# A quarter of the first layer of chunks 1 to 6 by Strassen's identity, with leaky results on VectorE

## Chip, core and metric

The kernel runs on one core of a Trainium2 chip. The metric is the device time of one execution in microseconds, median of several runs. The granted TensorE clock was 1.00 in the profiled execution.

## What is computed

Attention with 16 extra keys and values ("beacons") in front, for 8 batches of 8 heads (576 queries of 64 numbers), then a two-layer network on the joined heads (4608 tokens of 512 numbers, inner width 2048) with a leaky activation between the layers:

```
scores = scale * q @ concat(beacon_k, k).T      # causal behind the beacons
a = softmax(scores)
x = (a @ concat(beacon_v, v)) as 4608 x 512
h = x @ w_in                                    # 512 -> 2048, "first layer"
g = maximum(0.01 * h, h)
out = g @ w_out                                 # 2048 -> 512, "second layer"
```

## The kernel before

Tokens go through the network in nine chunks of 512. `g` below is a pair of heads (32 of them, four to a batch). For each pair the kernel loads q and k, turns them by DMA (`turn_pair`, on SP's queue), computes scores in tiles of 512 columns (`stretch`, L314, three tiles to a `block`), exponentials on ScalarE (L329, L333), zeroes the masked triangles on GpSimd (`triangle`, L289) and multiplies by the values (`value`, L359). VectorE then reads the value bank: a reciprocal (L388) and a multiplication (L389) that writes `x_nat`; `x_turn` (L417 to L426, SP's queue) turns that into `xT`, the first layer's input.

The first layer of a chunk is 16 calls of `up`, one for each 128 columns of `w_in`. Each calls `moe1` (L431): 4 matmuls of 512 columns (L442; in chunk 4, where `xT` wraps around, 8 of 256) into one bank, and ScalarE writes the leaky result to `gT` (L450).

The second layer of chunks 1 to 8 is done by Strassen's identity in Winograd's form, with 7 products of quarter matrices in place of 8. `token_sums` makes sums of parts of `gT` on VectorE, in two slices of 4 column groups (each four operations of 128x1024, run through `add_due` at L785); `weight_sums` makes those of `w_out` (L468 to L472). `down` calls `moe2` (L531), 14 calls to a chunk: two for each of the products 1, 4, 6, 2, 7, 5, 3, with 8 matmuls of 256 columns each (L544). `combine` (L563) adds the products up: ScalarE copies products 1, 4 and 5 out of their banks (L575), and VectorE does seven fp32 additions of 128x512 (L572). The buffers of `combine` (`p1`, `p4`, `p5`, `u2`, `u3`) exist once each. Two of the additions and one result are held back by two groups (`late`). `store` sends each quarter of the result to memory.

Chunks 7 and 8 (`TAIL` = 7) also do three quarters of the first layer by the same identity, in three rounds (`in_round`, L687): `in_product` (L651) computes one of seven products with 4 matmuls of 256 columns (L663). Their sums of weights are made by `w_in_sums` (L619) during chunk 6 and kept in `w_t` (for product 7 in place, in `w_in_sb`); their sums of `xT` by `x_in_sums` (L637).

The order of work is the program's own on every engine. The first eight pairs are written out as strings of steps (`run`, L930 to L938). After that a planner sorts events (blocks, values, turns, loads) by due time and puts groups of the network between them with `fill` (L767), which counts calls of `up` and `down`: a chunk's `up` calls start when its tokens are there, and from chunk 2 on they begin after the 14 `down` calls of the chunk before. `due` is a queue of VectorE operations that wait to be issued; each `up` and each `down` issues one of them (`add_due`).

All matmul results outside the score tiles go through the pool `ps_one`, four banks of 512 fp32 columns: the first layer's, the second layer's, the values' and the first of each block's three score tiles (which takes two banks). The other score tiles have the pool `ps_sc`. The banks of `ps_one` are handed out again in the order in which their last readers are issued.

Of the kernel before, what the change touches and what calls it, by code (L numbers as in the profile page):

```python
# [8 lines left out]
FP32 = mybir.dt.float32  # L9
# [6 lines left out]
def kernel(  # L16
# [93 lines left out]
    first_k = [  # L110
        sum_tile(2)[0:RP, 0:QK].bitcast(FP32).rearrange("p (i d) -> p i d", i=RI) for _ in range(2)
    ]
    k_nat0 = singles.tile([RP, RI, 2, D], BF16, name="k_nat0")
    bk_raw = singles.tile([128, B, D], FP32, name="bk_raw")
    bk = singles.tile([128, B, D], BF16, name="bk")

# [414 lines left out]
    def moe2(i, n2):  # L531
        if i == 0:
            moe2_plain(i, n2 // 4, n2 % 4)
            if n2 == NF - 1:
                weight_sums(1)
            return
        n, tile = PRODUCTS[n2 // 2], n2 % 2
        apart = i == NCH - 1 and n2 >= 10
        if tile == 0 or apart:
            banks["p"] = one_bank()  # L540
        acc = banks["p"]
        lo = 0 if apart else tile * HD
        for fc in range(HF):
            nc.tensor.matmul(  # L544
                out=acc[:, lo : lo + HD],
                lhsT=left(i, n, fc, tile),
                rhs=right(n, fc),
                start=(lo == 0 and fc == 0),
                stop=(fc == HF - 1),
                skip_group_check=True,  # L550
            )
        if apart:
            combine(i, n, acc[:, 0:HD], (tile, tile + 1))
        elif tile == 1:
            combine(i, n, acc, (0, 2))

    late = []

# [1 line left out]
        while late and (now or late[0][0] < done1[0] + done2[0]):  # L560
            late.pop(0)[1]()

    def combine(i, n, acc, tiles):  # L563
        lo, hi = tiles[0] * HD, tiles[1] * HD

        def part(name, new=False):
            if new and lo == 0:
                parts[name] = opool.tile([128, 512], FP32, name=name, bufs=1)
            return parts[name][:, lo:hi]

        def add(to, x, y):
            nc.vector.tensor_tensor(out=to, in0=x, in1=y, op=ADD)  # L572

        if n in (1, 4, 5):
            nc.scalar.copy(out=part(f"p{n}", True), in_=acc)  # L575
        if n == 6:
            add(part("u2", True), acc, part("p1"))
        elif n == 2:
            add(part("p1"), acc, part("p1"))
            store(i, 0, 0, tiles, part("p1"))  # L580
        elif n == 7:
            add(part("u3", True), acc, part("u2"))
            add(part("p4"), part("u3"), part("p4"))
            store(i, 1, 0, tiles, part("p4"))
        elif n == 5:
            u2, u3, p5 = part("u2"), part("u3"), part("p5")

            def rest():
                add(u3, u3, p5)
                store(i, 1, 1, tiles, u3)  # L590
                add(p5, u2, p5)

            late.append((done1[0] + done2[0] + 1, rest))
        elif n == 3:
            add_late(True)
            add(part("p5"), acc, part("p5"))
            store(i, 0, 1, tiles, part("p5"))

    def store(i, half, cols, tiles, c):
        t0 = i * 512 + half * HT + tiles[0] * 128  # L600
# [15 lines left out]
        for name, (t, lo) in zip(("p1", "p5", "u2", "u3", "c12", "c21", "c22"), temp_at)  # L616
    }

    def w_in_sums(n, lo=0, hi=ROUNDS, first=False):  # L619
        cols = slice(lo * 256, hi * 256)  # L620
        (b11, b21), (b12, b22) = (
            [w_in_sb[i][:, at : at + 2, cols] for at in (0, 2)] for i in range(2)
        )
        x, y = {5: (b12, b11), 6: (b22, w_t[5][:, :, cols]), 4: (b21, w_t[6][:, :, cols]), 7: (b22, b12)}[n]
        at = 0 if first else len(due)
        due[at:at] = [
            (TAIL - 1, dict(out=w_t[n][:, j, cols], in0=x[:, j], in1=y[:, j], op=SUB)) for j in range(2)
        ]

    def x_parts(i):  # L630
        at = i * 512 % (XR * S)
        assert at + 512 <= XR * S
        return [[xT[:, 2 * c : 2 * c + 2, at + r * HT : at + (r + 1) * HT] for c in range(2)] for r in range(2)]
# [16 lines left out]

    def in_product(i, n, r, bank, first):  # L651
        (a11, a12), (_, a22) = x_parts(i)
        x = {1: a11, 2: a12, 4: a22}.get(n)
        x = x_sums[i][n] if x is None else x
        for f in range(2):
            cols = slice(r * 256 + f, r * 256 + f + 255, 2)
            for j in range(2):
                if n in w_t:
                    w = w_t[n][:, j, cols]
# [12 lines left out]
    leaves = []  # L672

# [114 lines left out]
    def add_all(i):  # L788
        while due and due[0][0] == i:
            add_due()  # L790
# [123 lines left out]
    with order:  # L914
# [127 lines left out]
```

## Time and profile before

| what | value |
|---|---|
| time before, median of 3 runs | 326.06 us (324.29 to 326.34) |
| the profiled execution's own time | 325.64 us |
| its span, first to last instruction | 323.8 us |
| PE (TensorE) busy | 314.3 us, 97% of the span |
| PEld (its weight loads, beside the matmuls) | 219.1 us, 68% |
| DVE (VectorE) busy | 168.0 us, 52% |
| ACT (ScalarE) busy | 203.8 us, 63% |
| POOL (GpSimd) busy | 184.3 us, 57% |

L and a number is a line of the kernel. In groups of instructions the columns are line, engine, operation, output and inputs by the program's names, shapes, count, then busy microseconds and mean nanoseconds of one, then idle time of the engine just before them and what ended it. In a timeline the columns are start, duration, engine, line, operation, names, shapes and count, and in brackets the idle time before and what ended it. In a list of waits they are the waiting engine, tile and line, what it waited for, the total in microseconds, the number of times and the longest. In the strip of 40 slices each digit is the busy share of a slice in tenths.

### The profile page before, as it was taken

The page shows a single profiled execution, that of the slowest core. Times are in us where ns is not written, and L with a number is a line of the kernel's source. Part 1 is how long each engine was busy: PE and PEld are TensorE (multiplying, and loading weights), DVE is VectorE, ACT ScalarE, POOL GpSimd, SP SyncE. Part 2 cuts the span into 40 slices and gives each one's busy share as a digit, 9 for nine tenths or more (in the row PEclk, how much of TensorE's full clock was granted, in tenths as well). Part 3 has the DMA queues.
Part 4 walks back from the last instruction along what each step waited for, and adds up shares of the span by engine and source line. Part 5 has one row for each costly group of instructions (what it writes and reads, how often), then busy time and mean ns, then how long its engine had stood idle before and what let it go on. Part 6 is the DMA issues. An engine that isn't in the chain of part 4 may idle for free.

```text
span 323.8 us, 8701 instructions
## 1 busy us (share of the span) xinstructions
PE 314.3 (97%) x3468; PEld 219.1 (68%) x3494; DVE 168.0 (52%) x341; ACT 203.8 (63%) x346; POOL 184.3 (57%) x354
## 2 busy tenths in 40 slices
PE   7999999999999999999999999999999999999995
PEld 4575555444588557855788888656875697688784
DVE  3464245508255244444443454525464689577954
ACT  4968962387855786478746874687458547455510
POOL 8895868999996787659875977666221000000000
PEclk9999999999999999999999999999999999999999
DMA  8999999999999999999999999999222100200123
GB/s 137 129 189 192 124 214 140 169 177 188 135 152 160 216 138 129 114 186 97 141 176 174 99 143 119 188 128 129 44 81 82 26 2 32 75 25 2 65 67 130
DMA packets 155256, 39.78 MB, mean 123 GB/s; under 512 B 142368, under 2 KB 152480, under 8 KB 155216
## 3 DMA queue, kind: packets, MB, share of 16 engines
q0 software_dynamic: 99824, 18.54, 91.1%
q1 hardware_dynamic: 55120, 20.62, 38.3%
q8 instruction: 27, 0.44, 0.6%
q14 instruction: 13, 0.11, 0.1%
q10 hardware_dynamic: 272, 0.07, 0.1%
HBM read 37.22 MB, written 9.44 MB: 144 GB/s over the span
## 4 chain that ended last, share of the span: by engine, by line
PE 72%; DMA 14%; POOL 9%; ACT 3%; issue 1%; DVE 0%; POOLq 0%; ACTq 0%; SPq 0%
PE acc L442 24%; PE acc L544 19%; PE sc L544 11%; PE av L359 6%; PE sc L314 5%; PE acc L663 5%; DMA w_out_sb<-in_moe_w_out_dram 4%; DMA gsum<-in_k_dram 4%; POOL aT L289 3%; DMA k_nat<-in_k_dram 3%; DMA v_aug<-in_v_dram 2%; ACT aT L333 2%; DMA kT<-k_nat 2%; POOL gsum L158 1%; POOL v_aug L214 1%
## 5 line engine op out<-in xcount | busy, mean ns | idle before, releaser
L442 PE MATMUL acc<-xT,w_in_sb 128*128 128x512 bf16 (+1 forms) x537 | 116.5, 354 | 1.5 <-ACT aT L329 0.3
L450 ACT ACTIVATE gT<-acc 128x512 bf16<-128x512 f32 x124 | 70.8, 623 | 33.1 <-PE acc L442 32.6
L289 POOL TENSOR_SCALAR_AFFINE_SELECT aT<-aT 128x256 bf16<-128x256 bf16 (+2 forms) x160 | 59.7, 403 | 51.4 <-ACT aT L329 31.5
L442 PEld LDWEIGHTS <-w_in_sb 128*128 128x128 bf16 x560 | 51.7, 98 | 43.9 <-issue 2.9
L544 PEld LDWEIGHTS <-gT 128*128 128x128 bf16 x512 | 48.7, 98 | 7.7 <-issue 1.8
L333 ACT ACTIVATE aT<-sc 128x1024 bf16<-128x1024 f32 (+3 forms) x64 | 51.7, 892 | 0.0
L329 ACT ACTIVATE aT<-sc 128x512 bf16<-128x512 f32 (+3 forms) x64 | 29.0, 520 | 27.8 <-PE sc L314 27.8
L388 DVE RECIPROCAL rec<-av 128x6 f32<-128x6 f32 (+1 forms) x64 | 12.0, 187 | 65.0 <-PE av L359 64.4
L359 PEld LDWEIGHTS <-aT 128*128 128x128 bf16 (+1 forms) x960 | 36.9, 98 | 9.2 <-issue 1.4
L544 PEld LDWEIGHTS <-gsum 128*128 128x128 bf16 x384 | 36.5, 98 | 6.5 <-issue 0.4
L359 PE MATMUL av<-v_aug,aT 128*128 128x65 bf16 (+1 forms) x960 | 39.8, 194 | 0.8 <-DMA v_aug<-in_v_dram 0.4
L214 POOL DMA_DIRECT2D v_aug<-in_v_dram x40 | 34.1, 856 | 4.2 <-DMA w_in_sb<-in_moe_w_in_dram 3.8
L171 POOL DMA_DIRECT2D k_nat<-in_k_dram x48 | 34.8, 730 | 0.9 <-DMA w_out_sb<-in_moe_w_out_dram 0.3
L171 POOL DMA_DIRECT2D q_nat<-in_q_dram x48 | 34.8, 729 | 0.6 <-issue 0.4
L389 DVE TENSOR_TENSOR x_nat<-av,rec 128x384 bf16<-128x384 f32 (+1 forms) x64 | 31.4, 491 | 2.2
L544 PE MATMUL acc<-w_out_sb,gT 128*128 128x256 bf16 x240 | 28.9, 273 | 0.4 <-ACT gT L450 0.4
L276 ACT ACTIVATE aT<-sc 128x1024 bf16<-128x1024 f32 (+3 forms) x32 | 26.0, 874 | 4.7 <-PE sc L267 2.5
L314 PE MATMUL sc<-qT,kT 64*128 64x80 bf16 (+22 forms) x384 | 22.2, 250 | 0.3
L314 PEld LDWEIGHTS <-kT 64*128 64x128 bf16 x384 | 12.8, 94 | 11.2 <-issue 7.6
L544 PE MATMUL acc<-w_sum,gsum 128*128 128x256 bf16 x160 | 20.1, 273 | 0.0
L575 ACT COPY p<-acc 128x512 f32<-128x512 f32 x15 | 9.1, 604 | 16.8 <-PE acc L544 16.8
L785 DVE TENSOR_TENSOR gsum<-gT 128x1024 bf16<-128x1024 bf16 x16 | 11.0, 688 | 15.7 <-ACT gT L450 15.7
(95 smaller groups left out, 339.0 us busy)
## 6 DMA issues: line engine op xcount, KB each, us to landing
out_dram<-p SPq DMA_DIRECT2D x26, 256.0 KB, 3.2
q_nat<-in_q_dram POOLq DMA_DIRECT2D x48, 72.0 KB, 5.5
k_nat<-in_k_dram POOLq DMA_DIRECT2D x48, 72.0 KB, 5.3
v_aug<-in_v_dram POOLq DMA_DIRECT2D x24, 128.0 KB, 6.5
w_in_sb<-in_moe_w_in_dram POOLq DMA_DIRECT2D x2, 1024.0 KB, 12.4
w_out_sb<-in_moe_w_out_dram POOLq DMA_DIRECT2D x2, 1024.0 KB, 12.1
out_dram<-u SPq DMA_DIRECT2D x8, 256.0 KB, 2.7
gsum<-in_q_dram POOLq DMA_DIRECT2D x8, 144.0 KB, 7.1
```

The costliest lines, as they stand in the source:

```text
L171: nc.gpsimd.dma_start(out=t[:, :, par], in_=(q, k)[which][b, 2 * hp + par].rearrange("(t p) d -> p t d", p=NR),)
L214: nc.gpsimd.dma_start(out=dst[lo : ROWS[c], c, :, 0:D], in_=v[b, :, OFF[c] : OFF[c] + n].rearrange("h p d -> p h d"),)
L276: nc.scalar.activation(out=aT[:, :, c0 : c0 + w], in_=sc[:, :, 0:w], func=AF.Exp, scale=0.125)
L289: nc.gpsimd.affine_select(out=view, in_=view, compare_op=ALU.is_ge, fill=0.0, base=128 - n if lo == 0 else 0, channel_multiplier=-1, patte ...
L314: nc.tensor.matmul(out=(sc[par] if apart else sc[:, par])[:, at : at + b - a], lhsT=kT[ps_, c * 128 : (c + 1) * 128], rhs=qT[ps_, q0 : q0 ...
L329: nc.scalar.activation(out=probs[g][:, par, lo:hi], in_=sc[par][:, at : at + hi - lo], func=AF.Exp, scale=0.125)
L333: nc.scalar.activation(out=probs[g][:, :, lo:hi], in_=sc[:, :, at : at + hi - lo], func=AF.Exp, scale=0.125)
L359: nc.tensor.matmul(out=avv[:, n, 0 : D + 1], lhsT=aT[0 : ROWS[c], par, a0 : a0 + 128], rhs=va[0 : ROWS[c], c, 2 * hp + par, :], start=(c = ...
L389: nc.vector.tensor_tensor(out=x_nat[:, t0:t1].rearrange("p t e d -> p (t e) d"), in0=avv[:, :, 0:D], in1=rec[:, n0:n1, None].to_broadcast( ...
L442: nc.tensor.matmul(out=acc[:, lo:hi], lhsT=w_in_cols(fc, j), rhs=xT[:, j, x0 : x0 + hi - lo], start=(j == 0), stop=(j == NJ - 1), skip_gro ...
L450: nc.scalar.activation(out=gT[i][:, fc, :], in_=acc, func=AF.Prelu, alpha=0.01)
L544: nc.tensor.matmul(out=acc[:, lo : lo + HD], lhsT=left(i, n, fc, tile), rhs=right(n, fc), start=(lo == 0 and fc == 0), stop=(fc == HF - 1) ...
```

## The change

In chunks 1 to 6 the sixteen calls of `up` become twelve plain groups and four units (`mixed_unit`). The units do column groups 0, 1, 8 and 9 by the identity: products 1 and 4, then 6 and 2, then 7 and 5, then 3, each product 4 matmuls of 256 columns in a bank of `ps_one`. A unit is taken when the second layer of the chunk before is done and a plain group has gone between, or when four plain groups are left. The products are added up by `combine`, as in the second layer, and its results go through `leak`, one scalar_tensor_tensor on VectorE (0.01 times the value, maximum with the value) into `gT`. Four sums of `xT` per chunk are put into `due` at the chunk's first group; they are kept in the columns of `gT` that the last four plain groups write. The second layer's first slice of token sums is put into `due` after the last unit, the second after the last plain group.

The weight sums for these columns are made once, by `t2` at the end of the written-out steps (eight operations of 128x256), into a new tile `w_in_sum` (product 7 in place); `k_nat0` shares that tile. The tail's `w_in_sums` then leave out the first 256 columns, and its rounds take them from `w_in_sum`.

```diff
-    k_nat0 = singles.tile([RP, RI, 2, D], BF16, name="k_nat0")
+    w_in_sum = singles.tile([128, 3, 2, 256], BF16, name="w_in_sum")
+    k_nat0 = w_in_sum.rearrange("p n j f -> p (n j f)")[0:RP, 0 : RI * 2 * D].rearrange(
+        "p (i h d) -> p i h d", i=RI, h=2
+    )
...
-        if part == 0:
+        if part == 2:
+            for n in (5, 6, 4, 7):
+                w_in_sums(n, 0, 1)
+            add_all(TAIL - 1)
+        elif part == 0:
...
-            combine(i, n, acc, (0, 2))
+            combine(i, n, acc, (0, 2), store)
...
-    def combine(i, n, acc, tiles):
+    def combine(i, n, acc, tiles, put):
...
-            store(i, 0, 0, tiles, part("p1"))
+            put(i, 0, 0, tiles, part("p1"))
...
-    def w_in_sums(n, lo=0, hi=ROUNDS, first=False):
+    def w_in_sum_of(n, lo, hi):
+        if n != 7 and lo == 0:
+            assert hi == 1
+            return w_in_sum[:, (5, 6, 4).index(n)]
+        return w_t[n][:, :, lo * 256 : hi * 256]
+
+    def w_in_sums(n, lo=1, hi=ROUNDS, first=False):
...
     def x_in_sums(i):
         (a11, a12), (a21, a22) = x_parts(i)
-        s1, s2, s3, s4 = (
-            flat_a[t][:, lo : lo + X_COLS].rearrange("p (j t) -> p j t", j=2)
-            for t, lo in sum_at[4 * (i - TAIL) : 4 * (i - TAIL) + 4]
-        )
+        if i < TAIL:
+            at = [gT[i][:, fc] for fc in UPS[-4:]]
+        else:
+            at = [flat_a[t][:, lo : lo + X_COLS] for t, lo in sum_at[4 * (i - TAIL) : 4 * (i - TAIL) + 4]]
+        s1, s2, s3, s4 = (t.rearrange("p (j t) -> p j t", j=2) for t in at)
...
+    UPS = [2, 10, 3, 11, 4, 12, 5, 13, 6, 14, 7, 15]
+    UNITS = [(1, 4), (6, 2), (7, 5), (3,)]
+    ups_left, units_left, x_ops = {}, {}, {}
+
+    def leak(i, half, cols, tiles, c):
+        nc.vector.scalar_tensor_tensor(
+            out=gT[i][:, cols * HF : cols * HF + 2, half * HT : (half + 1) * HT],
+            in0=c.rearrange("p (f t) -> p f t", f=2),
+            scalar=0.01,
+            in1=c.rearrange("p (f t) -> p f t", f=2),
+            op0=ALU.mult,
+            op1=ALU.max,
+        )
+
+    def mixed_unit(i, n):
+        if n == 0:
+            ups_left[i], units_left[i] = list(UPS), list(UNITS)
+            gT[i] = gpool.tile([128, NF, 512], BF16, name="gT")
+            x_ops[i] = x_in_sums(i)
+            due.extend(x_ops[i])
+        ups, units = ups_left[i], units_left[i]
+        if units and at2[0] >= i and (len(ups) == 4 or len(ups) < len(UPS) - len(UNITS) + len(units)):
+            for p in units.pop(0):
+                while p in x_sums[i] and any(op is o for op in x_ops[i] for o in due):
+                    add_due()
+                bank = ps_one.tile([128, 512], FP32, name="acc", tag="one")
+                in_product(i, p, 0, bank, True)
+                combine(i, p, bank, (0, 2), leak)
+            if not units:
+                due.extend((i, op) for op in token_sums(i, 0, SLICE))
+        else:
+            moe1(i, ups.pop(0))
+            if not ups:
+                due.extend((i, op) for op in token_sums(i, SLICE, 2 * SLICE))
...
-        fc = n if i1 == 0 else n // 2 + n % 2 * HF
-        moe1(i1, fc)
+        mixed = 0 < i1 < TAIL
+        if mixed:
+            mixed_unit(i1, n)
+        else:
+            moe1(i1, n if i1 == 0 else n // 2 + n % 2 * HF)
         if (i1, n) == (TAIL - 1, 4 * (ROUNDS - 1) + 2):
-            w_in_sums(7, 0, ROUNDS - 1, first=True)
+            w_in_sums(7, 1, ROUNDS - 1, first=True)
             add_due()
...
-        if i1 and n % (2 * SLICE) == 2 * SLICE - 1:
+        if i1 and not mixed and n % (2 * SLICE) == 2 * SLICE - 1:
...
-        run("m7.1 m7.2 N9.1 u b8.2 b9.2 b10.2 b11.2 x6 v7.0 T9 v7.1 d d d N10.0 N10.1 d V2.0 V2.1 x7 t0 T10")
+        run("m7.1 m7.2 N9.1 u b8.2 b9.2 b10.2 b11.2 x6 v7.0 T9 v7.1 d d d N10.0 N10.1 d V2.0 V2.1 x7 t0 t2 T10")
```

More of the change, by code (lines that the diff above doesn't have):

```diff
@@ L552, in moe2 @@
         if apart:
-            combine(i, n, acc[:, 0:HD], (tile, tile + 1))
+            combine(i, n, acc[:, 0:HD], (tile, tile + 1), store)
         elif tile == 1:
-            combine(i, n, acc, (0, 2))
+            combine(i, n, acc, (0, 2), store)
     late = []
@@ L583, in combine @@
             add(part("p4"), part("u3"), part("p4"))
-            store(i, 1, 0, tiles, part("p4"))
+            put(i, 1, 0, tiles, part("p4"))
         elif n == 5:
@@ L589, in rest @@
                 add(u3, u3, p5)
-                store(i, 1, 1, tiles, u3)
+                put(i, 1, 1, tiles, u3)
                 add(p5, u2, p5)
@@ L596, in combine @@
             add(part("p5"), acc, part("p5"))
-            store(i, 0, 1, tiles, part("p5"))
+            put(i, 0, 1, tiles, part("p5"))
     def store(i, half, cols, tiles, c):
@@ L623, in w_in_sums @@
         )
-        x, y = {5: (b12, b11), 6: (b22, w_t[5][:, :, cols]), 4: (b21, w_t[6][:, :, cols]), 7: (b22, b12)}[n]
+        x, y = {
+            5: lambda: (b12, b11),
+            6: lambda: (b22, w_in_sum_of(5, lo, hi)),
+            4: lambda: (b21, w_in_sum_of(6, lo, hi)),
+            7: lambda: (b22, b12),
+        }[n]()
+        to = w_in_sum_of(n, lo, hi)
         at = 0 if first else len(due)
         due[at:at] = [
-            (TAIL - 1, dict(out=w_t[n][:, j, cols], in0=x[:, j], in1=y[:, j], op=SUB)) for j in range(2)
+            (TAIL - 1, dict(out=to[:, j], in0=x[:, j], in1=y[:, j], op=SUB)) for j in range(2)
         ]
     def x_parts(i):
-        at = i * 512 % (XR * S)
-        assert at + 512 <= XR * S
-        return [[xT[:, 2 * c : 2 * c + 2, at + r * HT : at + (r + 1) * HT] for c in range(2)] for r in range(2)]
+        at = [(i * 512 + r * HT) % (XR * S) for r in range(2)]
+        assert max(at) + HT <= XR * S
+        return [[xT[:, 2 * c : 2 * c + 2, at[r] : at[r] + HT] for c in range(2)] for r in range(2)]
     x_sums = {}
@@ L658, in in_product @@
                 if n in w_t:
-                    w = w_t[n][:, j, cols]
+                    w = w_in_sum_of(n, r, r + 1)[:, j, f : f + 255 : 2]
                 else:
```

## The prediction

> **What bounds the kernel now.** I read the page's first two parts, then TensorE's waits, then the instructions of TensorE and VectorE in the stretch where chunk 2's first layer runs (105 to 124 us), and last the groups by shape for durations.
>
> ```profile
> PE 314.3 (97%) x3468; PEld 219.1 (68%) x3494; DVE 168.0 (52%) x341; ACT 203.8 (63%) x346; POOL 184.3 (57%) x354
> ...
> PE   7999999999999999999999999999999999999995
> ...
> DVE  3464245508255244444443454525464689577954
> ```
>
> TensorE (PE) works in nearly every slice; VectorE (DVE) is half idle through the middle. PE's waits on other engines come to 4.1 us in all; the longest groups are:
>
> ```profile
> PE av L825 <- DVE blank L917: 1.1, 1, 1.1
> PE tp L243 <- DMA gsum<-in_q_dram: 0.8, 1, 0.8
> PE acc L519 <- DMA w_out_sb<-in_moe_w_out_dram: 0.5, 1, 0.5
> PE acc L544 <- ACT gT L450: 0.4, 2, 0.2
> ```
>
> So PE is the bound, and time is won only by fewer PE cycles, or lost by a wait put in front of PE. Whether VectorE's idle half is free where the change needs it is seen in chunk 2:
>
> ```profile
> 105.17 2.75 PE L442 MATMUL acc<-xT,w_in_sb 128*128 128x512 bf16 x11
> 107.76 0.53 PE L359 MATMUL av<-v_aug,aT 128*128 128x65 bf16 x12
> 108.13 1.89 PE L442 MATMUL acc<-xT,w_in_sb 128*128 128x512 bf16 x8
> 109.86 0.71 PE L359 MATMUL av<-v_aug,aT 128*128 128x65 bf16 x18
> 110.41 1.03 PE L442 MATMUL acc<-xT,w_in_sb 128*128 128x512 bf16 x4
> 111.37 0.83 PE L314 MATMUL sc<-qT,kT 64*128 64x400 bf16 x12
> ```
>
> ```profile
> 108.33 0.20 DVE L388 RECIPROCAL rec<-av 128x6 f32<-128x6 f32 x1 [2.27 <-PE av L359]
> ...
> 110.61 0.18 DVE L388 RECIPROCAL rec<-av 128x4 f32<-128x4 f32 x1 [1.49 <-PE av L359]
> 110.83 0.42 DVE L389 TENSOR_TENSOR x_nat<-av,rec 128x256 bf16<-128x256 f32 x1
> 115.89 0.69 DVE L785 TENSOR_TENSOR gsum<-gT 128x1024 bf16<-128x1024 bf16 x1 [4.64 <-ACT gT L450]
> ```
>
> VectorE's idle time stands in brackets: 2.27, 1.49 and 4.64 us, 8.4 us up to 115.9. The value results (L388, L389) free their bank only when VectorE has read them.
>
> **The change, part by part.** Durations:
>
> ```profile
> L785 DVE TENSOR_TENSOR aT<-xT 128x512 bf16<-128x512 bf16 x3 | 1.2, 416 | 0.0
> L572 DVE TENSOR_TENSOR p<-acc,p 128x512 f32<-128x512 f32 x10 | 6.9, 691 | 8.1 <-PE acc L544 7.9
> L575 ACT COPY p<-acc 128x512 f32<-128x512 f32 x15 | 9.1, 604 | 16.8 <-PE acc L544 16.8
> L450 ACT ACTIVATE gT<-acc 128x512 bf16<-128x512 f32 x124 | 70.8, 623 | 33.1 <-PE acc L442 32.6
> ```
>
> PE. Per chunk, 4 plain groups of 16 matmuls of 512 columns become 7 products of 4 matmuls of 256. From starts in the timeline, a plain group takes 108.13 to 109.86 for two, 0.867 each; eight 256-column matmuls take 0.875 (94.62 to 95.50). So 4 x 0.867 = 3.47 against 28 x 0.109 = 3.06: 0.41 us saved, 2.4 us in six chunks. That is all that can be won.
>
> Here the Trainium skill speaks against the change: "TensorE: Matmul & The Clock Gate", section "Back-to-back issue gap", gives sustained streams about 81 ns per matmul at 128 columns and 131 ns at 512, weight loads included. An estimate from these (98 ns at 256) makes 28 x 98 = 2.73 against 16 x 131 = 2.10 us, a loss of 3.8 us in six chunks. The rows above decide: 217 and 109 ns.
>
> ACT. Four leaky results (4 x 623 ns) become three copies (3 x 604): 0.7 us less per chunk. PE waited for ACT 1 us in all, so it is worth nothing by itself.
>
> VectorE, per chunk. Four token sums (416 ns, 1.66 us), seven fp32 adds (691 ns) and four leaky results with a scalar_tensor_tensor on 512 fp32 elements, which the trace does not show. Its nearest row is the fp32 add of the same shape, 0.69, which I take; below, the same rows start 0.60 apart when independent (101.24 to 101.88 and the like); above, two passes would be 1.38. Eleven such operations in a queue with their dependences (0.60 or 0.72 apart) take 7.4 us: with the sums 9 us, and all of it falls in the first 8 of a chunk's 16 groups.
>
> Where it falls. The planner counts groups, and its counts do not change, so order and interleaving stay as in the trace. There all 14 down products of chunk i-1 come before chunk i's first group (chunks 2 to 6), so the condition on the second layer holds at once: plain, (1,4), plain, (6,2), plain, (7,5), plain, (3), then eight plain. In chunk 1 the down products end after its fifth group, and the four units come in a row.
>
> A walk through chunk 2, on the trace's clock. VectorE: chunk 1's last add to 106.06; three sums to 107.27; head 13's first value half is ready at 108.35, to 109.13; fourth sum 109.45; (6,2) gives u2 110.05, p1 110.65, leaky 111.37; the second value half, ready at 110.65, now 111.92; (7,5) gives 112.52, 113.24, leaky 113.96; the late part 114.56, leaky 115.28, 115.88; (3) 116.60, leaky 117.32. PE finished (3) at 114.06: VectorE is 3.3 us behind, and the slice's second-layer sums, issued one per group, now stand in front of head 14's value: three to 119.33, value to 120.02. PE meets this at the four ps_one banks, which go round in the order in which their readers are issued. The score tile at 111.32 wants the bank of head 13's second half, free at 111.92: 0.65 lost. Head 14's value half and the next plain group lose 0.16 and 0.33 behind (7) and (3) (free 115.90 and 116.60). The plain group at 118.95 wants head 14's bank, free at 120.02: 1.1 lost. Sum 2.24, less the 0.41 saved: +1.8 us.
>
> The same walk by the same durations gives: chunk 1 +4.9 (four units in a row, two value halves behind them, and the 2.3 us weight sum of L472 just ahead), chunk 2 +1.8, chunk 3 +2.8, chunk 4 +2.3, chunk 5 +1.8, chunk 6 +1.8. Sum +15.4.
>
> Weight sums ("t2"): eight operations of 128x256 bf16, 282 ns by the group of the same shape on w_in_sb (L785, twice in the tail), 0.19 apart, 1.5 us, put between the sums of L468 to L470 and the copy at 61.63. That copy frees the bank that chunk 1's first group wants at 62.3: +0.7. Later the tail's sums shrink (six from 768 to 512 columns, 0.55 to 0.42; two from 512 to 256, 0.42 to 0.28): 1.1 us of VectorE, in the walk of chunk 6.
>
> Edits at no cost. Two scratch uses: the x sums lie in the gT columns of the last four plain groups, whose results ACT writes from about 120 us, 5 us after the products have read them; k_nat0 is read 40 us before w_in_sum is written. If a product were late there, ACT's results and then PE would wait for it. No DMA is added or moved. But x_turn's transposes wait in SP's queue for VectorE's x_nat, and behind them stand the next heads' qT and kT transposes (1.2 us each); a value 2 to 3 us late delays them as much. They are issued about two heads (15 us) ahead of use, which covers it; if not, each late microsecond is PE's. The tail's rounds only take their first quarter's weights from another tile: nothing.
>
> Sum: 15.4 + 0.7 = 16.1 us, on the profiled execution's 325.64 us (span 323.8): 341.7. The walk on the old order gives 1.6 us more of bank waits than the trace shows, so I take off 0.7: 341.0. The profiled run lies 0.4 below the median of 326.06, so the forecast is +15 us on that.
>
> **The rivals.** (1) The backlog is absorbed, the other side. PE loses nothing as long as VectorE frees a bank before it comes round, three allocations or about 2.6 us later. If the walk's lag of 3.3 to 5 us stays below that, only the saving remains: 325.64 - 2.4 = 323.2, with t2 and chunk 1 partly paid some 327. For it: at 262 to 280 us VectorE works without a gap and PE does not wait. Against: there the second layer's products lie in other banks, no value stands in VectorE's queue and the leaky results are ACT's.
>
> (2) The leaky operation is dear. At 1.38 us, 24 operations add 17 us of VectorE, and by the walk 14.6 us more of waits: 356. For it: one two-input sum (L472) took 2303 ns where three like it took 1215 to 1226. Against: that is still 1.1 ns per element, so 512 elements fit in 0.69.
>
> (3) VectorE slows under GpSimd, busy in 57% of the span. Sums of 691 ns reached 887 once. If all two-input operations took 0.89, the walk gives 4 us more: 345. Against: 10 of 11 of that group keep 0.68 to 0.69.
>
> (4) The change does not do what it says: the units come in a row in every chunk. Each chunk then costs chunk 1's 4.9: 325.6 + 29.4 + 0.7 = 356. Against: the trace's order of down and up groups.
>
> **How the numbers follow.** The forecast with (3) as its upper part 0.73; (1) 0.15; (2) and (4) together 0.08; half waits (banks freed sooner than walked, +5 to +8, 331 to 333) sit at the forecast's lower edge; 0.04 for what I have not seen. About 1% is what a measurement of this kernel can tell from no change: 322.8 to 329.3. (1) lies inside it, as 2.4 us is 0.7%, though near its lower end; of (1) and the unseen 0.04 I count 0.13 as same, 0.03 as faster and 0.03 as slower, which with 0.73 and 0.08 makes slower 0.84. The range 330 to 356 leaves out (1) and what lies beyond (2). The forecast's own range is 333 to 350.
>
> **What would show it.** Right: VectorE's busy time rises by about 55 us to 223; L442's matmuls fall by 96 of 512 columns or their halves; PE waits on x_nat (L389) and on L572's adds grow from 0.6 us to over 10, chiefly in the second quarter of each chunk's groups; ACT falls by 4 us; the tail from the last value on keeps its 67 us. Wrong: PE's waits stay under 3 us, the leaky row is far from 0.69, or chunk 1 does not lose the most.

## The result and the profile after

| what | value |
|---|---|
| time after, median of 6 runs | 337.76 us (336.42 to 343.11) |
| time before on the same chip, median of 6 runs | 324.82 us (324.04 to 326.34) |
| ratio, 95% interval | 1.0378 [1.0341, 1.0416] |
| the profiled execution's own time, its span | 338.16 us, 336.5 us (before 325.64, 323.8) |

The kernel became 3.8% slower; 341.0 was forecast, 3.2 us above the median. One remark on reading: the profiles of two experiments (`e3_leak_on_act`, `e7_from2_spread_bf16`) were taken in executions well above their medians, and nothing but the kind of a wait is read from the first, nothing at all from the second.

The page after, engines and strips (the columns are those of the page before):

```profile
PE 318.9 (95%) x3550; PEld 226.6 (67%) x3550; DVE 221.2 (66%) x439; ACT 201.0 (60%) x340; POOL 190.9 (57%) x354
...
PE   8999999895999999998999999999999999999995
...
DVE  3572455736764895469637984786559979757854
...
PEclk9999999998999999999999999999999999999999
```

VectorE works 53 us more (168.0 before), ScalarE 3 us less. PE has lost its even row of nines, most of all in slice 10 (about 76 to 84 us), a 5, which is also the only slice where the granted clock is below 9. The leaky operation, not in the trace of before, has two rows:

```profile
L697 DVE SCALAR_TENSOR_TENSOR gT<-p 128x512 bf16<-128x512 f32 x18 | 12.9, 717 | 0.6
L697 DVE SCALAR_TENSOR_TENSOR gT<-u 128x512 bf16<-128x512 f32 x6 | 4.3, 720 | 0.2
```

Where the 12.7 us of span went is read from the starts of PE's first matmul of each stretch in the two timelines:

| from | before | after | lost | walk of the prediction |
|---|---|---|---|---|
| start to chunk 1's first group | 62.27 | 61.71 | -0.6 | +0.7 |
| chunk 1 (to chunk 2's first group) | 42.90 | 49.07 | +6.2 | +4.9 |
| chunk 2 | 33.61 | 35.14 | +1.5 | +1.8 |
| chunk 3 | 33.25 | 35.14 | +1.9 | +2.8 |
| chunk 4 | 34.31 | 34.99 | +0.7 | +2.3 |
| chunk 5 | 33.62 | 35.14 | +1.5 | +1.8 |
| chunk 6 (groups only) | 17.51 | 18.34 | +0.8 | +1.8 |
| the rest to the end of the span | 66.33 | 66.97 | +0.6 | 0 |

The walk's order is there (chunk 1 loses by far the most, the others 1 to 2 us), but chunk 1 loses more and chunks 2 to 6 lose 6.4 us where 10.5 were walked.

PE's waits in the list after (total, number, longest):

```profile
PE sc L317 <- DVE x_nat L392: 2.0, 3, 0.8
PE sc L317 <- ACT p L582: 1.9, 1, 1.9
PE acc L445 <- DVE u L579: 1.4, 1, 1.4
PE acc L445 <- DVE p L579: 1.3, 3, 0.9
```

The whole list is 13.2 us, 4.1 before. That is less than the loss, and the reader should see why. A plain group starts 0.86 us before what follows it (110.78 to 111.64), but the timeline gives them 1.03 us: ends are modelled and overlap the next start by some 0.17. A wait therefore shows only what exceeds 0.17, and one below that does not show. The list has 21 waits after and 10 before; the 11 more hide some 11 x 0.17 = 1.9 us. With 1.4 us of low clock (below) and less the 2.4 us that the products should save, that makes 9.1 + 1.9 + 1.4 - 2.4 = 10.0 of the 12.7. I take the other 2.7 us for waits too short to be listed; they were not shown one by one.

**Chunk 2, the queue on VectorE.** Timeline of chunk 2's middle, VectorE and then PE:

```profile
121.38 0.89 DVE L579 TENSOR_TENSOR p<-u,p 128x512 f32<-128x512 f32 x1
122.37 0.69 DVE L579 TENSOR_TENSOR p<-acc,p 128x512 f32<-128x512 f32 x1
123.09 0.70 DVE L697 SCALAR_TENSOR_TENSOR gT<-p 128x512 bf16<-128x512 f32 x1
123.72 0.68 DVE L840 TENSOR_TENSOR gsum<-gT 128x1024 bf16<-128x1024 bf16 x1
124.43 0.69 DVE L840 TENSOR_TENSOR gsum<-gsum,gT 128x1024 bf16<-128x1024 bf16 x1
125.04 0.68 DVE L840 TENSOR_TENSOR gT<-gT 128x1024 bf16<-128x1024 bf16 x1
125.64 0.19 DVE L391 RECIPROCAL rec<-av 128x6 f32<-128x6 f32 x1
125.86 0.56 DVE L392 TENSOR_TENSOR x_nat<-av,rec 128x384 bf16<-128x384 f32 x1
```

```profile
119.42 0.60 PE L683 MATMUL acc<-gT,w_in_sb 128*128 128x256 bf16 x4
119.86 1.89 PE L445 MATMUL acc<-xT,w_in_sb 128*128 128x512 bf16 x8
121.80 0.53 PE L362 MATMUL av<-v_aug,aT 128*128 128x65 bf16 x12
...
126.47 0.85 PE L317 MATMUL sc<-qT,kT 64*128 64x64 bf16 x15 [0.75 <-DVE x_nat L392]
```

No VectorE row from 121.38 on has idle time in brackets. PE had finished product 3 at 119.86; VectorE's leaky result of it ends at 123.79, 3.9 us behind (3.3 in the walk). Head 14's value was ready at 122.3, stood behind product 3's two operations and three token sums, and its first half left its bank at 126.4. PE's score tile wanted that bank and waited 0.75 us.

**Chunk 1, something else.** Timelines of ScalarE, VectorE and PE:

```profile
78.61 0.58 ACT L582 COPY p<-acc 128x512 f32<-128x512 f32 x1 [3.55 <-DMA out_dram<-p]
```

```profile
81.25 0.69 DVE L579 TENSOR_TENSOR u<-acc,u 128x512 f32<-128x512 f32 x1 [2.61 <-DMA out_dram<-u]
```

```profile
79.25 0.84 PE L317 MATMUL sc<-qT,kT 64*128 64x96 bf16 x16 [1.92 <-ACT p L582]
80.01 0.61 PE L683 MATMUL acc<-gT,w_in_sb 128*128 128x256 bf16 x4
82.00 4.12 PE L445 MATMUL acc<-xT,w_in_sb 128*128 128x512 bf16 x12 [1.37 <-DVE u L579]
```

The copy of product 5 and the addition for product 7 do not wait for PE or for VectorE's queue, but for stores. Chunk 0's third and fourth output quarters lie in `p5` and `u3`, and their stores were issued on SP's queue at 73.04 and 77.46 us, the second behind a turn of q and one of k. In the old kernel nobody wanted these buffers until chunk 1's second layer; now a unit wants them at once. PE idles 1.92 and 1.37 us, and then a third loss follows: twelve matmuls take 4.12 us that take 2.77 at 127.26 us. The stretches give the granted clock in the column after the five engines:

```profile
81.00:82.00 1.00, 0.00 (x1) 0.00 (x1) 0.69 (x1) 1.00 (x2) 0.77 (x3) 0.69 1.80 147
82.00:83.00 1.00, 1.00 (x3) 0.40 (x3) 0.93 (x2) 0.80 (x1) 0.13 (x1) 0.50 3.32 66
83.00:84.00 1.00, 1.00 (x4) 0.30 (x2) 1.00 (x2) 0.10 (x1) 1.00 (x2) 0.50 0.08 7
84.00:85.00 1.00, 1.00 (x4) 0.40 (x3) 0.97 (x3) 0.50 (x1) 1.00 (x3) 0.60 1.35 187
```

The clock is 0.50 from before 82 to past 84 us: 4.12 - 2.77 = 1.4 us lost with PE at work.

Chunk 2 has a little of the same, because some buffers still hold chunk 1's results. ScalarE's copies of products 4 and 5 wait for stores there, 0.55 us and (at 117.85) 0.94 us, and PE's product 2 waits behind the first:

```profile
114.12 0.58 ACT L582 COPY p<-acc 128x512 f32<-128x512 f32 x1 [0.55 <-DMA out_dram<-p]
114.75 0.60 PE L683 MATMUL acc<-xT,w_in_sb 128*128 128x256 bf16 x4 [0.40 <-ACT p L582]
```

So in chunk 2, where 1.5 us were lost although 0.4 were saved on PE, the starts put 0.95 us at the score tile behind head 14's value, 0.40 at this product, 0.33 at head 14's value and the group after it, and 0.24 at head 13's score tile. VectorE's queue is the largest part, not the whole.

### The profile page after: what moved, and what is told of

Same layout as the page of the kernel before. It is cut to its first block, busy times and chain, and to the rows that moved or that the text cites. A ratio compares the mean times of both kernels' runs of the same rounds, so it can differ in the third digit from the quotient of the medians.

```text
span 336.5 us, 8974 instructions
## 1 busy us (share of the span) xinstructions
PE 318.9 (95%) x3550; PEld 226.6 (67%) x3550; DVE 221.2 (66%) x439; ACT 201.0 (60%) x340; POOL 190.9 (57%) x354
## 5 line engine op out<-in xcount | busy, mean ns | idle before, releaser
L445 PE MATMUL acc<-xT,w_in_sb 128*128 128x512 bf16 (+1 forms) x448 | 98.9, 360 | 3.9 <-DVE u L579 1.4
L292 POOL TENSOR_SCALAR_AFFINE_SELECT aT<-aT 128x256 bf16<-128x256 bf16 (+2 forms) x160 | 66.4, 442 | 57.8 <-ACT aT L332 34.4
L453 ACT ACTIVATE gT<-acc 128x512 bf16<-128x512 f32 x100 | 58.2, 618 | 36.2 <-PE acc L445 35.8
L445 PEld LDWEIGHTS <-w_in_sb 128*128 128x128 bf16 x448 | 42.0, 99 | 39.2 <-issue 8.9
L362 PE MATMUL av<-v_aug,aT 128*128 128x65 bf16 (+1 forms) x960 | 39.0, 194 | 0.5 <-ACT p L582 0.4
L582 ACT COPY p<-acc 128x512 f32<-128x512 f32 x33 | 19.4, 609 | 25.3 <-PE acc L551 17.7
L317 PE MATMUL sc<-qT,kT 64*128 64x80 bf16 (+22 forms) x384 | 23.5, 250 | 6.1 <-DVE x_nat L392 2.0
L317 PEld LDWEIGHTS <-kT 64*128 64x128 bf16 x384 | 13.7, 94 | 16.6 <-issue 9.8
L579 DVE TENSOR_TENSOR p<-acc,p 128x512 f32<-128x512 f32 x22 | 15.2, 691 | 10.1 <-PE acc L551 8.7
L579 DVE TENSOR_TENSOR p<-u,p 128x512 f32<-128x512 f32 (+1 forms) x29 | 20.0, 690 | 1.5
```

Source lines behind the costliest of these rows:

```text
L292: nc.gpsimd.affine_select(out=view, in_=view, compare_op=ALU.is_ge, fill=0.0, base=128 - n if lo == 0 else 0, channel_multiplier=-1, patte ...
L317: nc.tensor.matmul(out=(sc[par] if apart else sc[:, par])[:, at : at + b - a], lhsT=kT[ps_, c * 128 : (c + 1) * 128], rhs=qT[ps_, q0 : q0 ...
L362: nc.tensor.matmul(out=avv[:, n, 0 : D + 1], lhsT=aT[0 : ROWS[c], par, a0 : a0 + 128], rhs=va[0 : ROWS[c], c, 2 * hp + par, :], start=(c = ...
L445: nc.tensor.matmul(out=acc[:, lo:hi], lhsT=w_in_cols(fc, j), rhs=xT[:, j, x0 : x0 + hi - lo], start=(j == 0), stop=(j == NJ - 1), skip_gro ...
L453: nc.scalar.activation(out=gT[i][:, fc, :], in_=acc, func=AF.Prelu, alpha=0.01)
```

## The experiments

The theory, called 'backlog' in the expectations (the walk): VectorE gets so much work in the first half of a chunk's groups that values and products leave their banks late, and PE waits. The rivals tested: the products themselves cost it; one part (the leaky operation, the weight sums, the stores) is the cause and the queue is not. Ratios are to the kernel before, run beside each; an effect against the changed kernel is the difference of the ratios times 325 us.

**The products without VectorE's part.** ScalarE writes the leaky results straight from the banks of products 2, 7, 5 and 3; ScalarE's copies, all additions and VectorE's leaky operations of the units are left out, so those quarters of `gT` hold single products and not their sums.

```diff
-                combine(i, p, bank, (0, 2), leak)
+                q = {2: (0, 0), 7: (1, 0), 5: (1, 1), 3: (0, 1)}.get(p)
+                if q:
+                    leave(i, q[1] * HF, q[0], bank)
```

> Leaves out VectorE's part of the units: the products' sums and VectorE's leaky results are not made; ScalarE writes the leaky result of products 2, 7, 5 and 3 straight from their banks into the four quarters of gT (four instructions per chunk, as many as the plain groups had), products 1, 4 and 6 are read by nobody. The sums of xT, the weight sums of t2 and all matmuls stay. Theory 'backlog' (VectorE's queue holds the banks): the 12.7 us of loss nearly vanish; 2.4 us less PE work against up to 2.7 us of waits left by a walk of the queue, so 322.5 to 327 us, PE waits on VectorE under 2 us. Theory 'matmuls' (halved matmuls with their own weight loads cost more than the 109 ns seen in the second layer): stays above 330 us. Theory 'buffers' (units wait for the buffers that chunk 0's and the last chunk's results are still being stored from): also vanishes, since no buffer is used; it is told apart by the next kernel.

Measured: 326.57 us against 325.43, ratio 1.0053 [1.0015, 1.0092]. So 10.6 of the changed kernel's 12.3 us (0.0378 x 325) go with what is left out here, and the rival that the halved matmuls themselves are dear (above 330) fell. What is left out is more than VectorE's queue: ScalarE's three copies a chunk and their waits for stores go too, and the banks of products 1, 4 and 6 need no reader. The next kernels part these. The 2.4 us that the products save on PE are not won either. PE's timeline in this kernel:

```profile
114.99 1.89 PE L445 MATMUL acc<-xT,w_in_sb 128*128 128x512 bf16 x8
117.03 0.53 PE L362 MATMUL av<-v_aug,aT 128*128 128x65 bf16 x12
117.52 1.89 PE L445 MATMUL acc<-xT,w_in_sb 128*128 128x512 bf16 x8
```

Eight matmuls need 8 x 0.217 = 1.73 us, so the value could start at 116.72 and starts 0.31 later; the next group starts 0.12 later than it could. ScalarE is at its exponentials from 114.52 to 116.5 and then has a queue of leaky results, so banks come free when it is done with the block, however early PE was. Chunk 2's groups take 18.18 us here, 18.15 in the old kernel: the 0.39 us by which PE was ahead at 114.99 are waited off by the chunk's end. ScalarE has four leaky results of the units per chunk here, where the changed kernel has three copies, so this wait need not be the changed kernel's own.

**No leaky operation, and twice.** First, the last addition of each quarter writes `gT` itself and the leaky operation is left out (the result lacks the activation there); second, it is done twice.

```diff
 # e10_no_leak
-            add(part("p1"), acc, part("p1"))
+            to = part("p1") if put is store else quarter(i, 0, 0)
+            add(to, acc, part("p1"))
...
 # e8_leak_twice
+        for _ in range(2):
+            nc.vector.scalar_tensor_tensor(
...
```

> Leaves out the leaky operation of the four quarters: the last addition of each quarter writes gT directly, so VectorE has 24 operations of 0.717 us (17.2 us) less. Theory (VectorE's queue in the first half of a chunk is what PE loses to, by length of the queue): the doubled leak cost 10.7 us for 16.6 us more, so one leak less is worth 6 to 10 us: 328 to 332. Rival (the loss comes from the banks that the additions hold, the leaky operation itself stands behind them and delays nothing): within 1 us of the changed kernel, 336.5 to 338.5.

> Each leaky instruction of the units is issued twice on VectorE (the same result twice): 24 x 0.69 = 16.6 us more of VectorE, nothing else. Theory 'backlog': the walk gives 14.6 us more, 24 operations that stand in front of values and second-layer sums with the banks already late; I expect 9 to 15 us: 347 to 353. Theory 'elsewhere' (the loss is made by waits for stores, by ScalarE and by the clock, and VectorE has room left): under 341.

Measured: 330.81 against 325.94, ratio 1.0161 [1.0113, 1.0209], and 348.44 against 325.90, ratio 1.0696 [1.0653, 1.0739]. Both lie in the theory's range. In one row:

| kernel | VectorE busy, us | ratio |
|---|---|---|
| before | 168.0 | 1 |
| products only | 176.4 | 1.0053 |
| no leaky operation | 204.8 | 1.0161 |
| the change | 221.2 | 1.0378 |
| leaky operation twice | 238.0 | 1.0696 |

The loss bends upward: the step with the 28 us of additions costs 3.5 us, the 16 us of leaky operations on top of them 7, the next 17 us 10, each give or take 2 us by the intervals. The starts in the four timelines say where. The table has the time of a chunk's groups up to its second layer, for chunk 1 up to chunk 2's first group. The profiled executions without the leaky operation and with it twice lie 1.7 us below and 1.9 us above their medians, so the table tells better where the loss is than how large:

| chunk | 1 | 2 | 3 | 4 | 5 | 6 |
|---|---|---|---|---|---|---|
| before | 42.90 | 18.15 | 17.78 | 18.47 | 18.16 | 17.51 |
| no leaky operation | 46.59 | 18.41 | 18.28 | 18.45 | 17.76 | 18.34 |
| the change | 49.07 | 19.68 | 19.68 | 19.14 | 19.67 | 18.34 |
| leaky operation twice | 48.40 | 24.58 | 20.37 | 20.70 | 20.29 | 19.86 |

Without the leaky operation chunks 2 to 5 lose 0.3 us together, where the change loses 5.6 there. Chunk 5 is even 0.40 us shorter than before: the products' saving can be won when the banks come free in time. What is left of the loss, 3.7 us, stands in chunk 1. So with the additions alone VectorE keeps up in chunks 2 to 5, and with the leaky operation behind them it does not: a queue with some slack, not a fixed price per operation. The last step is not the queue's alone, though. Of the 12.2 us by which the span grows from the change to the leaky operation done twice, 4.9 stand in chunk 2, and nearly all of these are one wait for a store (PE 3.08 us behind ScalarE's copy of product 5) and a granted clock of 0.50 from 124 to 126 us, after it:

```profile
121.82 0.58 ACT L582 COPY p<-acc 128x512 f32<-128x512 f32 x1 [3.51 <-DMA out_dram<-p]
122.46 0.81 PE L317 MATMUL sc<-qT,kT 64*128 64x400 bf16 x11 [3.08 <-ACT p L582]
```

**The leaky operation in bf16.** The last addition writes bf16 into `gT` and the leaky operation works there in place, to see if 2-byte operands make it faster.

```diff
+            to = part("p1") if put is store else quarter(i, 0, 0)
+            add(to, acc, part("p1"))
...
+        nc.vector.scalar_tensor_tensor(out=c, in0=c, scalar=0.01, in1=c, op0=ALU.mult, op1=ALU.max)
```

> The last addition of each quarter writes its bf16 result straight into gT, and the leaky instruction works there in place, bf16 in and out: the results are rounded before the leak and not after it. If the instruction then runs at two elements per cycle as the bf16 sums do (512 columns in 0.42 us), VectorE is relieved of 24 x 0.27 = 6.5 us and theory 'backlog' gives 5.2 us less by the walk, some 3 to 5 us: 333 to 335. If it stays at 0.69, the time stays within 1 us of 338, apart from fp32 buffers that come free earlier. Theory 'elsewhere': no change in either case.

Measured: 337.67 against 325.90, ratio 1.0352 [1.0306, 1.0397], not told apart from the change, and its row says why:

```profile
L706 DVE SCALAR_TENSOR_TENSOR gT<-gT 128x512 bf16<-128x512 bf16 x24 | 17.1, 714 | 0.8
```

714 ns against 717: this operation gains nothing from bf16, where plain sums of 128x512 do (691 ns in fp32, 416 in bf16). The additions here are those of the kernel without the leaky operation, so the 6.2 us between the two (0.0191 x 325) go with the operation itself and not with the buffers that the additions write.

**The leaky operation on ScalarE.**

```diff
-        nc.vector.scalar_tensor_tensor(
+        nc.scalar.activation(
...
+            func=AF.Prelu,
+            alpha=0.01,
```

> The leaky results of the units are written by ScalarE (Prelu from the same fp32 buffers) instead of VectorE: 24 x 0.69 us = 17 us leave VectorE, 24 x 0.63 us = 15 us go to ScalarE. Theory 'backlog': with 7 instead of 11 operations in its queue VectorE frees the banks earlier; the walk gives 1.9 us less: 335 to 336.5. Theory 'buffers': nothing changes, 337.5 to 338.5. If ScalarE's queue becomes the new wait (the score tiles' exponentials stand in it), slower: over 339.

Measured: 344.26 against 325.43, ratio 1.0579 [1.0543, 1.0614]: 6.5 us worse than the change, though VectorE has 17 us less to do. ScalarE's list of waits names it (total, number, longest):

```profile
ACT gT L697 <- DVE p L579: 18.9, 12, 6.9
```

The leaky result now stands in ScalarE's queue in front of plain results and exponentials and waits there for VectorE's additions. The walk's 335 to 336.5 us did not come; the rival that was written down beside it (a new wait on ScalarE) holds. In this order of work the leaky results are better left on VectorE, dear as they are there.

**Token sums later.** The first slice's four sums enter the queue four plain groups later (chunks 1 to 5).

```diff
-            if not units:
+            if not units and i == TAIL - 1:
                 due.extend((i, op) for op in token_sums(i, 0, SLICE))
...
+            if len(ups) == 4 and i < TAIL - 1:
+                due.extend((i, op) for op in token_sums(i, 0, SLICE))
```

> The first slice of the second layer's sums of tokens is queued four plain groups later (chunks 1 to 5), so that no sum of 0.69 us stands ahead of the third head's value on VectorE. Theory of the walk (three sums in front of that value cost 1.1 us a chunk): 4 to 5 us less, 333 to 334. Rival (the value is late because of the products' own additions, the sums hardly add to it): within 1.5 us, 336.3 to 338.5.

Measured: 335.07 against 325.94, ratio 1.0302 [1.0262, 1.0341], 2.5 us less than the change; the two intervals just touch. The wait at 126.47 is gone and with it most of its group:

```profile
PE sc L317 <- DVE x_nat L392: 0.4, 1, 0.4
```

2.0 us in 3 waits became 0.4 in one. The place was right and its size was half of what was written down: 2.5 us over five chunks are 0.5 a chunk, not 1.1. By the starts the chunks differ: 0.8 us are won in chunks 2 and 5, 0.4 in chunk 3 and none in chunk 4.

**Two plain groups between units.** Instead of one, in chunks 1 to 5.

```diff
-        if units and at2[0] >= i and (len(ups) == 4 or len(ups) < len(UPS) - len(UNITS) + len(units)):
+        if units and at2[0] >= i and (len(ups) == 4 or len(UPS) - len(ups) > (2 if i < TAIL - 1 else 1) * (len(UNITS) - len(units))):
```

> In chunks 1 to 5 two plain groups go between the units instead of one (units at the 2nd, 5th, 8th and 11th group; chunk 1 as far as its second layer allows; chunk 6 as before). The same instructions, spread over 11 groups instead of 8. Theory 'backlog': VectorE catches up between the units; the walk gives 4.5 us less: 333 to 335.5. Theory 'elsewhere': as before, 337 to 338.5; if the total of VectorE's work counts and not where it stands, also no change.

Measured: 334.30 against 325.90, ratio 1.0258 [1.0222, 1.0294], 3.9 us less than the change with the same work on every engine. By the starts in its timeline the groups of chunks 2, 3 and 5 now take 18.42, 18.06 and 18.43 us (19.68, 19.68 and 19.67 in the change; 18.15, 17.78 and 18.16 before): about 0.3 us of loss left in each. Chunk 4 got worse, 20.57 against 19.14, with two waits:

```profile
184.60 1.03 PE L445 MATMUL acc<-xT,w_in_sb 128*128 128x256 bf16 x8 [1.29 <-ACT gT L453]
196.71 1.05 PE L445 MATMUL acc<-xT,w_in_sb 128*128 128x256 bf16 x8 [0.79 <-DVE x_nat L392]
```

So in chunks 2, 3 and 5 the loss is one of bunching, not of the sum of work.

**Chunk 1.** Three kernels: chunk 1 plain as before, with the sums of `w_in` among its second layer; chunk 0's third and fourth output quarters in a buffer of their own; and that with the sums of `w_in` queued in chunk 1.

```diff
 # e2_from_chunk_2
-        mixed = 0 < i1 < TAIL
+        mixed = 1 < i1 < TAIL
...
 # e1_other_buffers, and in e11_buffers_and_t2
...
+                if t == 2:
+                    banks["o"] = sum_tile(2)
+                osb = banks["o"][:, (t - 2) * 2 * DM : (t - 1) * 2 * DM].bitcast(FP32)
...
 # e11_buffers_and_t2
+            if i == 1:
+                for p in (5, 6, 4, 7):
+                    w_in_sums(p, 0, 1)
...
```

> Chunk 1 stays plain and the weight sums of t2 are spread over the second layer of chunk 1; chunks 2 to 6 as changed. Chunk 1 lost 6.2 us by the starts of the chunks in the two traces, so both theories give 338 - 6.2 = about 331.5 us (330.5 to 333). If the losses of chunks 2 to 6 (1.5, 1.9, 0.7, 1.5 and 0.8 us, 6.4 in all, from the traces) were only late consequences of chunk 1's delay, say of transfers out of step, they would shrink too and the time would be under 328.

> Chunk 0's third and fourth token tile are put into a buffer of the token sums instead of p5 and u3, so that chunk 1's units need not wait for their stores; nothing else changes. Theory 'buffers': the two waits for stores in chunk 1 (3.6 us of ScalarE, 2.6 us of VectorE) and the drop of the granted clock to 0.5 behind them were most of chunk 1's 6.2 us, so 4 to 5.5 us are won back: 332.5 to 334. Theory 'backlog': chunk 1's four units in a row and the weight sum of 1.5 to 2.3 us ahead of them keep PE waiting anyway; by the walk chunk 1 then still loses 4.9 us, so 0.5 to 1.5 us are won back: 336.5 to 337.5.

> Chunk 0's third and fourth output quarters in a buffer of their own, and the eight sums of w_in queued in chunk 1 instead of standing in a row ahead of chunk 1's first group. Theory (chunk 1 loses 3.6 us to the stores and a low clock after them, and t2 costs 0.7 to 2.5 us of its own): 333 to 334.8. Rival (the eight sums cost nothing where they were; only the buffers count): 335.7 to 336.5, as with the buffers alone.

Measured: ratios 1.0252 [1.0216, 1.0287], 1.0336 [1.0307, 1.0365] and 1.0351 [1.0315, 1.0387]. Without the change in chunk 1 the kernel is 4.1 us faster than with it, so about a third of the loss is chunk 1's (by the starts of the profiled execution chunk 1 takes 43.57 us there, 5.5 less). Chunks 2 to 5 take 19.74, 19.68, 19.14 and 19.68 us in it, as in the change: their loss is their own and no late consequence of chunk 1, and the rival of under 328 us fell. Buffers of their own take both store waits out of chunk 1 (its groups up to the second layer: 20.26 us in the change, 16.53 and 17.41 with the buffers, 14.94 before), but the medians win only 1.4 and 0.9 us, and the intervals overlap that of the change: 336.09 lies between what the two theories said of the second kernel, 336.73 beside the rival's end for the third, and 333.94 us for the first is 0.9 above what was expected. Part of the difference is seen. In the second kernel's profile PE waited 1.50 us for the weight sums near 60 us, after which the granted clock was 0.50 from 62 to 65 us and eight matmuls of 512 columns took far longer than 0.217 each; in the third's, chunk 1's second layer waited for a turn of k:

```profile
100.47 0.50 PE L317 MATMUL sc<-qT,kT 64*128 64x256 bf16 x6 [1.42 <-DMA kT<-k_nat]
```

(0.67 at this place in the change, at 102.42). The turn's data came 1.95 us earlier than in the change and PE 1.95 + 0.75 = 2.7 us earlier, so PE waited off 0.75 of what it had won. Moving the sums of `w_in` made no difference that can be told (336.73 and 336.09, overlapping intervals).

**Remedies together.** Own buffers, sums of `w_in` queued in chunk 1, and spread units; and then chunk 1 plain, spread units and bf16.

> The buffers of chunk 0 apart, the sums of w_in queued in chunk 1, and two plain groups between units in chunks 1 to 5 (all three together). If the three remedies act on separate places: 337.8 less 1.7 (buffers) less 3.5 (spread) less 0.7 (sums) = 331.9, between 330.5 and 333. If they act on the same place (chunk 1): no better than the spread alone, 334 to 334.5. Either way above the kernel before, since the products alone were worth nothing.

> Three of the edits together: chunk 1 plain with the weight sums in its second layer, units spread in chunks 2 to 5, leaky results in bf16 in place. By what chunk 1 gave alone (333.9) and the walk's 6.1 us for the other two, 328 to 330 us if theory 'backlog' is right about them. Below the kernel before (325.4) only if all waits vanish, since at most 5 x 0.41 = 2 us of PE work is saved; I do not expect it.

Measured: 331.71 against 325.94, ratio 1.0223 [1.0179, 1.0267], and 330.10 against 325.90, ratio 1.0134 [1.0093, 1.0174]. The remedies add up roughly as written down (the second ended 0.1 us above its range), and the best of them still loses 1.3%. No version tried beats the kernel before, and there is little to be uncovered: nothing was won with all of VectorE's part taken away, and the 0.40 us of chunk 5 without the leaky operation, six times over, would be 2.4 us.

## Why the prediction was right, and where not

- *PE bound, so a wait in front of PE decides.* Right: PE lost 12.7 us of span while its own matmuls cost what was computed (chunk 2 was 0.39 us ahead by 114.99 us in the products-only kernel; 0.41 was computed).
- *2.4 us "is all that can be won".* The bound held, and the change wins nothing of it. Only chunk 5 of the kernel without the leaky operation shows it, 0.40 us where 0.41 was computed. The first rival's price of 323.2 did not come even with VectorE's part left out (326.57), and its mechanism (the backlog is absorbed) fell. The stretch it drew on, VectorE without a gap from 262 to 280 us, has two gaps of 0.2 us and ends at 279.2, which changes nothing.
- *The leaky operation at 0.69.* Right: 0.717. The second rival (1.38) fell with it.
- *VectorE slowed by GpSimd (third rival).* Partly there: in chunk 2, additions of 0.89 and a leaky operation of 0.78 us stand among rows of 0.69; the mean of the additions `u<-u,p` rose from 731 to 771 ns, that of `p<-acc,p` stayed at 691. Whether GpSimd is the cause was not tested.
- *Units in a row in every chunk (fourth rival).* Fell: only in chunk 1, as the timeline of chunk 2 shows plain groups between the units.
- *The backlog: +1.8, +2.8, +2.3, +1.8, +1.8 for chunks 2 to 6.* The mechanism was right: the lag of 3.9 us against 3.3 walked, the value behind three sums, the bank that PE meets late, the win from moving the sums or spreading the units, and the rise with VectorE's work. The term was too large, 10.5 where 6.4 were lost. The step that was mis-sized is the price of the waits: the score tile of head 13 started at 117.64, 0.09 late where 0.65 was walked, and the token sums were worth 0.5 us a chunk (0.8 in chunk 2) where 1.1 was walked. The walk also left out ScalarE: in chunk 2 its copies, late for stores, cost 0.40 us, and head 14's value and the group after it came 0.33 late at its queue, as in the kernel with the products only. A deduction for it had been seen (the same walk on the old order gave 1.6 us too much) but only 0.7 were taken off.
- *Chunk 1, +4.9 from four units in a row, two value halves and L472's weight sum.* The size was near (6.2) and the cause incomplete: the step that failed is "Edits at no cost", which looked at the scratch uses and at the queue of turns, and not at `p5` and `u3`, which exist once each and still held chunk 0's results for their stores. Nor did the head start of the turns cover all, as that step said: the score tile at 102.42 waited 0.67 us for a turn of k. The weight sum itself, 2.30 us before, took 1.53 and ran ahead of the units' additions. How the 6.2 us divide is settled only in part: with own buffers 1.6 and 2.5 us of loss stay in chunk 1's groups, but of the rest the medians gave back only about 1 us.
- *t2, +0.7.* Its wait is there (0.94 us for `w_in_sum` at the score tile before chunk 1's first group, in the kernel with later token sums), but not in the time: chunk 1 began 0.56 us earlier than before, and moving the sums changed no median. The kernel with chunk 1 plain has no `t2` there and waits 0.92 us at the same tile, for `w_sum`. In the experiments' profiles chunk 1 begins anywhere from 60.5 to 66.6 us, so this first stretch varies by more than the term.
- *What would show it.* VectorE's 223 us (221.2), 4 us less on ScalarE (3) and the tail's 67 us (66.97) were right. That the waits on `x_nat` and on the additions grow from 0.6 to over 10 us was wrong by its measure: 2.5 and 2.9 us in the list after, and the 0.6 was of PE's weight loads, as PE's own list before has no wait on `x_nat`. Late banks were met in many small pieces, which this list does not hold, and through ScalarE's copies.

The right sum thus came from a term that was 4 us too large, another that was 1.3 us too small with a wrong cause, and 0.7 that did not reach the time. That it came within 3.2 us of the median is in part luck: the errors have both signs.

## What to carry to other kernels

A saving on the bound engine is worth something only if the engines that empty its banks can follow at once; here the products alone, 2.4 us shorter on PE, ended no earlier, and one chunk whose banks came free in time kept its 0.40 us. Work put on a half-idle engine is priced by the queue where it falls: the same operations cost 3.9 us less when spread out, and chunks 2 to 5 lost 0.3 us with the additions alone, 5.6 with the leaky operations behind them. When buffers are used in a new place, ask when their last reader (a store in a DMA queue, too) lets them go there.

## What the runs showed of the hardware

- The granted clock of PE fell to 0.50 after short gaps. In the change, from 77 to 82 us PE was busy 1.70 of 5 us, in pieces between gaps of 1.92 and 1.37 us; the clock was 0.50 from before 82 to past 84 us and 1.00 from 85 on. The Trainium skill, "TensorE: Matmul & The Clock Gate", section "Why this matters for your kernels", asks for no idle gap over about 3 us between bursts of matmuls. By that rule these two gaps should have been harmless. Nor is a pair needed: with own buffers for chunk 0 the clock was 0.50 from 62 to 65 us after one gap of 1.50 us that ended at 60.58, and with the leaky operation twice it was 0.50 from 90 to 92 us after one of 1.72 us that ended at 88.34. One of 1.42 us (at 100.47, with own buffers and the sums queued) and a pair of 1.23 and 1.08 us (at 79.88 and 86.11, without the leaky operation) left it at 1.00. What decides between them no run here shows.
- A scalar_tensor_tensor of 512 elements takes 717 ns from fp32 inputs and 714 ns with all operands in bf16. The Trainium skill, "VectorE: DVE Perf Modes", section "What auto-detection actually checks", states that a two-source tensor_tensor reaches a doubled rate when every tensor is 16-bit; this case's plain sums do (416 against 691 ns), and this other two-source operation does not.
